# MLP matmuls in four column tiles wherever a stretch of TensorE work also holds values or sums

## The chip, the cores and the metric

The kernel runs on one core of a Trainium2 chip, in one launch. The metric is the device time of an execution in microseconds (us). Engines are named as in the profile: PE is TensorE's matmul, PEld its weight load, ACT is ScalarE, DVE is VectorE, POOL is GpSimd, SP is SyncE.

## The reference

Attention with a few extra "beacon" keys, then an MLP with a gate. There are 8 batches of 8 heads, 576 positions, 16 beacon keys and head size 64; the MLP goes from 512 to 2048 and back to 512 over 4608 tokens. Inputs and the output are float32.

```
scores = q @ concat(beacon_k, k)^T / 8        # causal over k, beacons always seen
a      = exp(scores - max) / (sum + 1e-9)
x      = a @ concat(beacon_v, v)              # per head, then heads side by side: [4608, 512]
h      = x @ w_in
out    = (h * sigmoid(1.702 * h)) @ w_out
```

## The kernel before, in words

All matmul operands are float16. Attention is worked in 16 sets of four heads (`NSET`; a set is half of a batch's heads). The MLP is worked in 10 groups of tokens: two of 256 and eight of 512 (`GROUPS`).

**Three shapes of the array.** TensorE takes a matmul's stationary operand as rows x columns of the array, which the profile prints in front of the moving operand's shape:

- scores (`e_qk`, L434), mode "r": 32 rows by 128 columns. The four heads of a set lie in four groups of 32 partitions, so that four such matmuls fill the array.
- values and sums (`e_av`, L521), mode "c": 128 rows by 32 columns. The four heads write four groups of 32 output partitions of one PSUM tile, so that four such matmuls, a set, fill the array. Sums use a tile of ones as their weights.
- MLP, mode "m": 128 rows by 128 columns. The first layer (`e_m1`, L580) has 512 moving columns in the groups of 512 tokens (256 in the first two groups and where a group crosses the end of the ring buffer `xT`). The second layer is `e_m2` (L625, 512 columns) in the first two groups, and `e_prod` (L694, 256 columns) in the eight others, where it is seven products of quarter matrices that DVE adds up (`e_s`, L645, before; `e_join`, L710, after).

**Order of the work.** Every operation, such as one score visit or one tile of the MLP, is an `Op` of a planner, with its engine, its dependencies and its mode. The order on each engine is written out by hand in the lists `ORDER`; `Plan.run` only merges these lists by start times that it reckons, and hands out the four PSUM tiles `u` as they come free. The function's last loop then emits the operations in that order. There are 55 score visits on TensorE; the scores have a single PSUM tile (`s`), so a visit has to wait until ACT has taken the exponential of the visit before (`e_exp`, L445). Between two visits TensorE works on MLP operations, on values and sums, or on both.

**Around it.** POOL and DVE mask the exponentials (L466, L459), DVE adds parts of the sums up (L484), turns sums into reciprocals (`e_z1`, `e_z2`, L533 to L544) and scales the values into `xT` (`e_norm`, L556). DVE also transposes q and k for the scores (`e_turn`, L405). ACT applies the gate to the first layer (`e_gelu`, L601; in the first two groups tanh on ACT, L594, and DVE, L613). POOL issues the loads, SP the stores.

Of the kernel before, what the change touches and what calls it, by code (L numbers as in the profile page):

```python
# [195 lines left out]
def kernel(  # L196
# [11 lines left out]
    nc = tc.nc  # L208
# [7 lines left out]
    P = 128  # L216
# [8 lines left out]
    NKT = DMODEL // P  # L225
    NNT = DFF // P
# [21 lines left out]
    HM, HN = 256, NNT // 2  # L248
# [71 lines left out]
    for s in range(EARLY, NSET):  # L320
        c = 0
# [14 lines left out]
    def ring_tile(key):  # L336
        if key not in rings:
            i = plan.tiles[key]
            rings[key] = psu.tile([P, 512], F32, tag=f"u{i}", name=f"u{i}")
        return rings[key]  # L340
# [225 lines left out]
        GROUPS.append((t, min(NTOK, t + 512)))  # L566
    NG = len(GROUPS)

    def e_m1(g, n0, n1):
        t0, t1 = GROUPS[g]  # L570
        w = t1 - t0
        if g not in gts:
            gts[g] = gp.tile([P, NNT, 512], F16, tag="g", name="g")
        u = ring_tile(("m1", g, n0))
        for nt in range(n0, n1):
            o = (nt - n0) * w
            cut = max(t0, t1 // XR * XR)
            for a, e in ((t0, cut), (cut, t1)):
                for kp in range(NKT if a < e else 0):
                    nc.tensor.matmul(  # L580
                        u[:, o + a - t0 : o + e - t0],
                        w1t[:, kp, nt * P : (nt + 1) * P],
                        xT[:, kp, a % XR : (e - 1) % XR + 1],
                        start=(kp == 0),
                        stop=(kp == NKT - 1),
                    )

    sigs = {}
# [33 lines left out]
    def e_m2(g, mt, qt):  # L622
        o = ring_tile(("m2", g, mt))
        for nt in range(4 * qt, 4 * qt + 4):
            nc.tensor.matmul(  # L625
                o[:, :],
                gts[g][:, nt, mt * P : (mt + 1) * P],
                w2t[:, nt, :],
                start=(nt == 0),
                stop=(nt == NNT - 1),  # L630
            )

    osbs = {}
# [13 lines left out]
    def tb(i):  # L647
        if i < 3:
            return tB[i][:, :, :]
        return w2t[:, 0:HN, HM:]  # L650
# [14 lines left out]
    def quarter(g, i, j):  # L665
        return gts[g][:, HN * j : HN * (j + 1), HM * i : HM * (i + 1)]
# [13 lines left out]
    def e_prod(g, p, n0, n1):  # L680
        u = ring_tile(("p", g, p))
        w = lambda i, j: w2t[:, HN * i : HN * (i + 1), HM * j : HM * (j + 1)]
        lhs, rhs = {
            1: (quarter(g, 0, 0), w(0, 0)),
            2: (quarter(g, 0, 1), w(1, 0)),
            3: (sA[2], w(1, 1)),
            4: (quarter(g, 1, 1), tb(2)),
            5: (sA[0], tb(0)),
            6: (sA[1], tb(1)),
            7: (quarter(g, 1, 0), tb(3)),  # L690
        }[p]
        for n in range(n0, n1):
            for mt in range(2):
                nc.tensor.matmul(  # L694
                    u[:, HM * mt : HM * (mt + 1)],
                    lhs[:, n, mt * P : (mt + 1) * P],
                    rhs[:, n, :],
                    start=(n == 0 and mt == 0),
                    stop=(n == HN - 1 and mt == 1),
                )  # L700

    def e_half(g, p, dst):
# [236 lines left out]
    def products(g):  # L939
# [17 lines left out]
        def prod(p):  # L957
            prev = []
            for n0 in range(0, HN, SQ):
                deps = list(prev)  # L960
                if lhs[p] is not None:
                    deps.append(sd[(lhs[p], n0)])
                else:
                    deps += [gates[(g, n + (HN if p in (2, 4) else 0))] for n in range(n0, n0 + SQ)]
                if rhs[p] is not None:
                    deps.append(tds[rhs[p]])
                o = op(
                    "PE", 2 * SQ * 109, deps, lambda n0=n0: e_prod(g, p, n0, n0 + SQ), kind="m2", pr=g,
                    ring=("p", g, p), mode="m", name=f"m2.{g}.{p}.{n0}",
                )  # L970
                prev = [o]
            last[p] = prev[0]
            done.setdefault(g, []).append(prev[0])
# [31 lines left out]
    def mlp(g):  # L1005
# [16 lines left out]
        for n0 in firsts:  # L1022
            n1 = n0 + n
            key = ("m1", g, n0)
            pe = op(
                "PE", 4 * n * (w / 2.4 + 2.8), xs + w1_of[n0] + old, lambda n0=n0, n1=n1: e_m1(g, n0, n1),
                kind="m1", pr=g, ring=key, mode="m", name=f"m1.{g}.{n0}",
            )
            m1s.setdefault(g, []).append(pe)
            if g >= GEL:  # L1030
                gates[(g, n0)] = op(
                    "ACT", 480, [pe], lambda n0=n0, n1=n1: e_gelu(g, n0, n1),
                    pr=1, closes=key, name="gelu", table="g",
                )
                continue
            a = op(
                "ACT", 480, [pe] + tanhs[-1:] + gated[-3:-2], lambda n0=n0, n1=n1: e_tanh(g, n0, n1),
                pr=1, name="tanh", table="e",
            )
            tanhs.append(a)  # L1040
            gates[(g, n0)] = op(
                "DVE", 606, [a], lambda n0=n0, n1=n1: e_gate(g, n0, n1), pr=2, closes=key, name="gate"
            )
            gated.append(gates[(g, n0)])
# [3 lines left out]
        for mt in range(w // P):  # L1048
            key = ("m2", g, mt)
            prev = None  # L1050
            for qt in range(4):
                deps = [gates[(g, n0)] for n0 in range(0, NNT if mt else 4 * qt + 4, n)] + [w2_ld[qt], prev]
                prev = op(
                    "PE", 4 * 215.8, deps, lambda g=g, mt=mt, qt=qt: e_m2(g, mt, qt), kind="m2",
                    pr=g, ring=key, mode="m", name=f"m2.{g}.{mt}.{qt}",
                )
                m2s[(g, mt, qt)] = prev
            done.setdefault(g, []).append(prev)
            ev = op("ACT", 480, [prev], lambda g=g, mt=mt: e_evac(g, mt), pr=1, closes=key, name="evac")
            op("SP", 60, [ev], lambda g=g, mt=mt: e_store(g, mt), name="store")  # L1060
# [20 lines left out]
    def also(o, d):  # L1081
        o.deps.append(d)
        o.left += 1
        d.users.append(o)

    for o in done.get(NPL - 1, []) + done.get(NPL - 2, []) if tds else ():
        also(tds[3], o)
    order = plan.run()
    for o in order:
        o.emit()  # L1090

# [28 lines left out]
```

The softmax here doesn't subtract the row's maximum and nothing guards it: scores larger than these inputs give would overflow.

## Time and profile before

| | |
|---|---|
| time, median of 3 runs | 330.57 us (330.24 to 332.09) |
| span of the profiled execution (first to last instruction) | 328.1 us; the profile gives no other time for it |
| TensorE matmuls and weight loads | 4288 each |
| of these: scores, values and sums, MLP | 1376, 1248, 1664 |
| mean granted TensorE clock | 1.000 |
| L580, first layer: busy, count | 130.4 us, 704 |
| ACT's gate L601: busy, count | 70.5 us, 128 |
| ACT's exponential L445: busy, count | 98.9 us, 66 |

The span runs from the first instruction to the last; a run's time is somewhat longer than the span. "Busy" is the union of an engine's instructions. The records of TensorE's matmuls overlap, since one streams in while the last drains and their ends are modelled: a matmul's cost is read from the distance to the next one's start, not from its duration. In the chain of work that ended last, each piece was released by the one before it.

### The profile page before, as it was taken

How to read it: one execution, taken by the hardware profiler on the slowest of the kernel's cores; microseconds unless marked ns; L12 is line 12 of the kernel's file. 1: busy time of each engine (PE TensorE's matmuls, PEld its weight loads, DVE VectorE, ACT ScalarE, POOL GpSimd, SP SyncE). 2: the span in 40 equal slices, each digit the busy share in tenths (PEclk: the TensorE clock that was granted, in tenths of full speed). 3: DMA queues.
4: the chain of work that ended last, by engine and by line, in shares of the span. 5: the costliest groups of instructions: out<-in, count | busy, mean ns of one | idle time of the engine just before them, and what ended most of it. 6: DMA issues, size and time to landing. Idle time of an engine off the chain costs nothing.

```text
span 328.1 us, 9811 instructions
## 1 busy us (share of the span) xinstructions
PE 309.3 (94%) x4288; PEld 210.0 (64%) x4288; DVE 235.9 (72%) x478; ACT 202.0 (62%) x236; POOL 114.0 (35%) x178
## 2 busy tenths in 40 slices
PE   0489999999999999999999999999999999999995
PEld 0367665544775467745878878547764776447884
DVE  3657788777987989977998798958557843006674
ACT  1567597687767686679767686868477212674010
POOL 8765487190319312951078019400042000000000
PEclk9999999999999999999999999999999999999999
DMA  7999999194424921693029809600120012000122
GB/s 126 161 202 209 203 187 181 34 99 103 113 67 72 186 50 34 70 191 57 2 45 177 133 2 122 157 0 2 37 96 2 2 34 78 18 0 2 65 98 97
DMA packets 58219, 28.81 MB, mean 88 GB/s; under 512 B 41280, under 2 KB 53568, under 8 KB 58176
## 3 DMA queue, kind: packets, MB, share of 16 engines
q0 software_dynamic: 47552, 18.49, 47.8%
q1 hardware_dynamic: 10560, 9.69, 9.1%
q8 instruction: 33, 0.54, 0.7%
q14 instruction: 10, 0.08, 0.1%
q10 hardware_dynamic: 64, 0.01, 0.0%
HBM read 37.22 MB, written 9.44 MB: 142 GB/s over the span
## 4 chain that ended last, share of the span: by engine, by line
PE 89%; ACT 4%; DVE 3%; DMA 2%; issue 1%; POOL 0%; DVEq 0%; ACTq 0%; POOLq 0%
PE u L580 36%; PE u L694 30%; PE s L434 9%; PE u L521 9%; PE u L625 4%; ACT E L445 3%; DMA qn<-in_q_dram 2%; DVE qT L405 1%; DVE sA L645 1%; DVE xT L556 1%; DVE rz L544 0%; DVE zt L533 0%; ACT L601 0%; DVE osb L710 0%; DVE rc L540 0%
## 5 line engine op out<-in xcount | busy, mean ns | idle before, releaser
L580 PE MATMUL u<-xT,w 128*128 128x512 f16 (+1 forms) x704 | 130.4, 340 | 0.5 <-ACT g L601 0.5
L445 ACT ACTIVATE E<-s 128x2048 f16<-128x2048 f32 (+5 forms) x66 | 98.9, 1515 | 46.0 <-PE s L434 45.6
L601 ACT ACTIVATE g<-u 128x512 f16<-128x512 f32 x128 | 70.5, 598 | 53.8 <-PE u L580 53.4
L580 PEld LDWEIGHTS <-w 128*128 128x128 f16 x704 | 67.8, 98 | 53.9 <-issue 1.5
L466 POOL TENSOR_SCALAR_AFFINE_SELECT E<-E 128x512 f16<-128x512 f16 (+3 forms) x78 | 49.3, 663 | 113.4 <-ACT E L445 81.6
L710 DVE SCALAR_TENSOR_TENSOR osb<-u,osb 128x512 f32<-128x512 f32 x56 | 37.2, 682 | 24.7 <-PE u L694 22.4
L694 PEld LDWEIGHTS <-g 128*128 128x128 f16 x512 | 48.4, 98 | 9.3 <-issue 0.2
L694 PE MATMUL u<-w,g 128*128 128x256 f16 x384 | 50.6, 273 | 0.0
L434 PE MATMUL s<-qT,kT 32*128 32x32 f16 (+20 forms) x1376 | 35.4, 232 | 14.4 <-DVE qT L405 8.4
L434 PEld LDWEIGHTS <-kT 32*128 32x128 f16 x1376 | 25.8, 94 | 30.6 <-issue 15.0
L694 PEld LDWEIGHTS <-sA 128*128 128x128 f16 x384 | 36.3, 98 | 5.3 <-issue 0.3
L694 PE MATMUL u<-tB,sA 128*128 128x256 f16 x256 | 35.0, 273 | 0.1
L645 DVE TENSOR_TENSOR sA<-g 128x512 f16<-128x512 f16 x32 | 12.9, 415 | 26.2 <-ACT g L601 26.2
L556 DVE TENSOR_TENSOR xT<-u,rz 128x352 f16<-128x352 f32 (+2 forms) x52 | 25.6, 517 | 6.9 <-PE u L521 6.7
L365 POOL DMA_DIRECT2D vb<-in_v_dram x32 | 27.4, 874 | 2.3 <-DMA kn<-in_k_dram 1.5
L521 PE MATMUL u<-E,vb 128*32 128x352 f16 (+8 forms) x928 | 28.0, 267 | 0.0
L484 DVE TENSOR_TENSOR zs<-zs,E 128x1344 f16<-128x1344 f16 (+2 forms) x36 | 22.7, 633 | 5.3 <-POOL E L466 4.4
L521 PEld LDWEIGHTS <-vb 128*32 128x32 f16 (+1 forms) x928 | 20.2, 99 | 5.9 <-issue 1.7
L405 DVE STREAM_TRANSPOSE kT<-kn 128x576 f32<-128x576 f32 x16 | 20.1, 1258 | 2.4 <-DMA kn<-in_k_dram 1.6
L405 DVE STREAM_TRANSPOSE qT<-qn 128x576 f32<-128x576 f32 x16 | 19.8, 1239 | 0.1
L533 DVE STREAM_TRANSPOSE zt<-u 128x224 f32<-128x224 f32 (+2 forms) x32 | 14.9, 471 | 6.6 <-PE u L521 6.5
L484 DVE TENSOR_TENSOR zs<-E 128x1856 f16<-128x1856 f16 x12 | 15.8, 1319 | 3.3 <-POOL E L466 3.3
(44 smaller groups left out, 237.7 us busy)
## 6 DMA issues: line engine op xcount, KB each, us to landing
out_dram<-osb SPq DMA_DIRECT2D x36, 256.0 KB, 2.5
kn<-in_k_dram POOLq DMA_DIRECT2D x16, 288.0 KB, 6.7
qn<-in_q_dram POOLq DMA_DIRECT2D x16, 288.0 KB, 6.6
vb<-in_v_dram POOLq DMA_DIRECT2D x24, 128.0 KB, 6.6
w<-in_moe_w_in_dram POOLq DMA_DIRECT2D x8, 256.0 KB, 9.9
w<-in_moe_w_out_dram POOLq DMA_DIRECT2D x4, 512.0 KB, 14.2
vb<-in_v_dram POOLq DMA_DIRECT2D x8, 112.0 KB, 5.0
vb<-in_v_dram POOLq DMA_DIRECT2D x8, 80.0 KB, 7.9
```

What stands on the lines that cost most here:

```text
L365: nc.gpsimd.dma_start(out=t[0 : hi - lo, j, h0:h1, :], in_=v[b, h0:h1, lo:hi, :].rearrange("h n d -> n h d"),)
L405: nc.vector.transpose(out=f32(dst.rearrange("p n e -> p (n e)")).rearrange("p (r t) -> p t r", t=TR), in_=f32(src[:, :]).rearrange("p (t c ...
L434: nc.tensor.matmul(sc[:, h, o : o + w], kT[s % NB2][r : r + 32, j * P : (j + 1) * P, d], qT[s % NB2][r : r + 32, a : a + w, d], start=(d = ...
L445: nc.scalar.activation(out=Es[s][:, :, c0:c1], in_=ss[i][:, :, o : o + c1 - c0], func=AFT.Exp, scale=0.125,)
L466: nc.gpsimd.affine_select(out=blk, in_=blk, compare_op=ALU.is_ge, fill=0.0, base=off + (Nb if j == 0 else 0), pattern=[[0, Q], [1, w]], ch ...
L484: nc.vector.tensor_tensor(out=t, in0=E[:, :, Z0:S] if i == 1 else t, in1=E[:, :, wcol[i] : wcol[i] + S - a], op=ALU.add,)
L521: nc.tensor.matmul(u[32 * h : 32 * h + 32, a:e], lhs, src[0:kw, h, col : col + e - a], start=first, stop=last,)
L556: nc.vector.tensor_tensor(out=xT[:, 2 * hs + x : 2 * hs + x + n, t0 : t0 + w], in0=rings[("av", s, x, half)][:, 0 : n * w].rearrange("p (n ...
L580: nc.tensor.matmul(u[:, o + a - t0 : o + e - t0], w1t[:, kp, nt * P : (nt + 1) * P], xT[:, kp, a % XR : (e - 1) % XR + 1], start=(kp == 0) ...
L601: nc.scalar.activation(out=gts[g][:, n0:n1, 0:w], in_=rings[("m1", g, n0)][:, 0 : n * w].rearrange("p (n w) -> p n w", n=n), func=AFT.Gelu ...
L694: nc.tensor.matmul(u[:, HM * mt : HM * (mt + 1)], lhs[:, n, mt * P : (mt + 1) * P], rhs[:, n, :], start=(n == 0 and mt == 0), stop=(n == H ...
L710: nc.vector.scalar_tensor_tensor(out=osbs[(g, dst)][:, :], in0=rings[("p", g, p)][:, :], scalar=scale_of(g), in1=osbs[(g, src)][:, :], op0 ...
```

## The change

MLP matmuls go through a new helper `mm`. With its flag set, it issues one matmul as four, one for each group of 32 output partitions: the weights' columns are cut into four, and each part meets the same moving operand. The flag is set for an MLP operation if the stretch of TensorE's order between two score visits in which it stands holds values or sums too (mode "c"). The work behind the last score visit counts as one such stretch. All else is emitted as before, in the same order.

```diff
+    tiled = [False]
+
+    def mm(o, lhs, rhs, start, stop):
+        if not tiled[0]:
+            nc.tensor.matmul(o, lhs, rhs, start=start, stop=stop)
+            return
+        for r in range(0, P, 32):
+            nc.tensor.matmul(o[r : r + 32], lhs[:, r : r + 32], rhs, start=start, stop=stop)
+
...
-                    nc.tensor.matmul(
+                    mm(
                         u[:, o + a - t0 : o + e - t0],
                         w1t[:, kp, nt * P : (nt + 1) * P],
                         xT[:, kp, a % XR : (e - 1) % XR + 1],
-                        start=(kp == 0),
-                        stop=(kp == NKT - 1),
+                        kp == 0,
+                        kp == NKT - 1,
                     )
...
     order = plan.run()
+    split, visit = set(), []
+    for o in [o for o in order if o.eng == "PE"] + [None]:
+        if o is None or o.mode == "r":
+            if any(x.mode == "c" for x in visit):
+                split.update(x.seq for x in visit if x.mode == "m")
+            visit = []
+        else:
+            visit.append(o)
     for o in order:
+        tiled[0] = o.seq in split
         o.emit()
```

The matmul calls in `e_m2` (L625) and `e_prod` (L694) are put through `mm` in the same way.

More of the change, by code (lines that the diff above doesn't have):

```diff
@@ L624, in e_m2 @@
         for nt in range(4 * qt, 4 * qt + 4):
-            nc.tensor.matmul(
+            mm(
                 o[:, :],
@@ L628, in e_m2 @@
                 w2t[:, nt, :],
-                start=(nt == 0),
-                stop=(nt == NNT - 1),
+                nt == 0,
+                nt == NNT - 1,
             )
@@ L693, in e_prod @@
             for mt in range(2):
-                nc.tensor.matmul(
+                mm(
                     u[:, HM * mt : HM * (mt + 1)],
@@ L697, in e_prod @@
                     rhs[:, n, :],
-                    start=(n == 0 and mt == 0),
-                    stop=(n == HN - 1 and mt == 1),
+                    n == 0 and mt == 0,
+                    n == HN - 1 and mt == 1,
                 )
```

## The prediction

> **What bounds the kernel now.** I read the page's busy rows and slices first, then its chain of work that ended last, then the timeline of TensorE alone, then the waits that TensorE ends.
>
> ```profile
> span 328.1 us, 9811 instructions
> ...
> PE 309.3 (94%) x4288; PEld 210.0 (64%) x4288; DVE 235.9 (72%) x478; ACT 202.0 (62%) x236; POOL 114.0 (35%) x178
> ...
> PE   0489999999999999999999999999999999999995
> ...
> PEclk9999999999999999999999999999999999999999
> ...
> PE 89%; ACT 4%; DVE 3%; DMA 2%; issue 1%; POOL 0%; DVEq 0%; ACTq 0%; POOLq 0%
> ```
>
> TensorE is busy in every slice after the first two, at the full granted clock, and 89% of the chain is TensorE work. A change in TensorE's time therefore reaches the end nearly one for one, except where another engine already holds TensorE up. The timeline of TensorE shows what the change touches:
>
> ```profile
> 130.87 0.60 PE L694 MATMUL u<-tB,sA 128*128 128x256 f16 x4
> 131.40 0.64 PE L434 MATMUL s<-qT,kT 32*128 32x384 f16 x24
> 131.97 1.61 PE L521 MATMUL u<-E,vb 128*32 128x224 f16 x56
> 133.51 1.05 PE L694 MATMUL u<-tB,sA 128*128 128x256 f16 x8
> 134.49 0.65 PE L434 MATMUL s<-qT,kT 32*128 32x320 f16 x24
> ...
> 150.19 4.49 PE L580 MATMUL u<-xT,w 128*128 128x512 f16 x20
> 154.52 1.04 PE L694 MATMUL u<-w,g 128*128 128x256 f16 x8
> 155.49 0.38 PE L521 MATMUL u<-zs,ones 128*32 128x352 f16 x8
> 155.69 0.23 PE L521 MATMUL u<-E,ones 128*32 128x80 f16 x8
> 155.85 0.61 PE L694 MATMUL u<-tB,g 128*128 128x256 f16 x4
> ```
>
> The first column is the start; the second column's end includes a modelled pipeline tail, so I use differences of starts. Three shapes of the array take turns: scores (L434, 32*128), values and sums (L521, 128*32) and MLP (L580, L625, L694, 128*128). Record by record, successive MLP matmuls of one run start 109 ns apart at 256 columns and 216 ns at 512: columns / 2.4 plus 2.5 ns.
>
> **What a change of shape costs.** From 154.52, eight MLP matmuls last 8 x 109 = 874 ns, but L521 starts after 970: 96 ns for the change. Over the whole trace the 15 changes from MLP to values cost 93 to 94 ns each, and the first set behind one runs 10 ns over its usual pitch: 104. From values to MLP (26 changes) it is 94 to 98 ns behind the fourth matmul of the last set (one is 106), and the first MLP matmul's pitch is 10 ns long as well: 107. Check on the 56 at 131.97: 14 sets of four with 3,328 columns are 1,387 ns at 2.4 columns per ns, some 44 for 14 pitches and 10 for the first; L694 starts after 1,540, so 99 are left, plus the 10.
>
> **Part 1, changes removed.** Following TensorE's timeline from end to end, there are 52 stretches between score visits with other work; 28 hold both MLP and values or sums, and inside these are the 41 changes above. They all go: 15 x 104 + 26 x 107 = 4.3 us. The changes at the two ends of a stretch stay (85 to 97 ns in every combination). In 20 of the 28 the last work is MLP; its fourth column tile now starts 10 ns behind its first, as L521's does: +0.2 us. Gross: **4.1 us**.
>
> **Part 2, matmuls added.** The 28 stretches hold 1,188 of the 1,664 MLP matmuls (404 of 512 columns, 784 of 256), among them all 408 behind the last values, where no change of shape is left to save. Each becomes four of 32 output rows: 3,564 matmuls and as many weight loads more. The nearest row is L521, which already runs this shape. Its four matmuls of a set start within 10 ns, and the next set starts columns / 2.4 plus 2 to 3 ns later: 149 to 150 ns at 352, 89 at 208, 49 at 112. The MLP pitch is columns / 2.4 plus 2.5. I take **0** per matmul. Not shown by any row: 512 columns in this shape, four tiles that read the same moving rows, and hundreds of sets in a row. The bound below is 0.5 ns less (0.6 us in all), the lower end of L521's 2 to 3 ns; above, the sets that follow an 80-column one (5 to 7 ns over, so +5 each, 5.9 us), and the supply of instructions, priced below as a rival. I take 0 because the sets of 208 to 352 columns are the nearest in width.
>
> Weights: four loads per set instead of one. In the 112-column sets four loads hide inside 49 ns, so they hide inside 109. If that cover failed, the 60 ns of room in a 256-column set would be the first to go.
>
> A rule against this change: the Trainium skill, "TensorEngine Tiling (Array Packing)", section Instruction Overhead, gives each matmul some 60 cycles of overhead and advises tiling for small dimensions only, which the MLP has not. Summed over four at 2.4 GHz that is an estimated 100 ns per set; were it added to the stream rather than hidden, 75 ns more for each of 1,188 matmuls, 89 us. The 49 ns sets of four say that it isn't added.
>
> Semaphores: in L521's sets only the fourth matmul carries the update; I expect the same, at no cost. The order of all engines is fixed by the ORDER lists and the planner's inputs are untouched, so no DMA, queue or buffer moves. The score operations, ACT, DVE and POOL instructions are the same.
>
> **Part 3, savings that another wait takes.** A score visit has one PSUM tile, so it cannot start before the last exponential ended. Where it did wait, it starts 51 or 52 ns after that end; where it starts later than that, the difference is slack.
>
> ```profile
> 83.01 0.55 DVE rz L544
> ...
> 86.69 0.44 DVE xT L556
> 87.14 0.04 issue
> 87.18 1.03 PE u L694 x8
> ...
> 91.75 1.89 ACT E L445
> 93.63 0.04 issue
> 93.67 0.65 PE s L434 x21
> ```
>
> In these pieces of the chain, ACT sets the start at 93.67: both changes saved in the stretch before it (0.21 us) only lengthen that wait. Scores at 49.59, 99.35, 102.11 and 195.73 start 111, 117, 195 and 84 ns after their exponential, 60, 65, 145 and 33 of slack against savings of 105, 105, 210 and 105: 0.22 us lost. Elsewhere behind mixed stretches the slack covers the saving. The DVE chain up to 87.18 starts from values at 80.9, so the two changes between are lost too (0.21). At 37.24 the scores wait for DVE's transposition of q; the change of shape behind the last values before it is lost, and DVE's idle 0.17 us ahead of that chain caps two more: together 0.2. Sum: **0.85 us** taken back, 3.3 left. At the end, six changes sit in the last stretch, from 241 on, where no other engine holds TensorE for more than 0.1 us; the last DVE join and the store follow as before.
>
> **Sum.** 328.1 - 3.3 = 324.8 us of span. The profile gives that execution no other time than its span; the median of the runs is 330.57, 2.5 more, for what lies around it. 324.8 + 2.5 = **327.3 us**, 1.0% faster.
>
> **Rivals.**
> *Waits take it back.* DVE is busy 36.5 of 40 us from 100 to 140, and the median slack ahead of a score visit is about 250 ns. If tighter waits on DVE and ACT absorb everything before 241, six changes remain: 0.6 us, 330.0. For it: the five clipped visits. Against: TensorE's own waits sum to under 2 us after 20.
>
> *Slower: the supply of instructions.* A 256-column set now takes 8 instructions in 109 ns, 13.6 ns each, through stretches as long as 11 us. The densest 256 instructions on record took 4.27 us from 56.5, 16.7 ns each. If that were the ceiling, a set would take 133 ns: 24.4 x 784 = 19 us more, less 3.3: 346. The 512-column sets (27 ns each) stay clear. It decides the sign from 13.6 + 3300 / 784 / 8 = 14.2 ns per instruction. Against it: TensorE's closing drain was reached with 33 instructions still to start, so some 33 are queued ahead; 192 instructions in 2.14 us from 229.3 then needed (192 - 33) per 2.14 us, 13.5 ns, and 128 in 1.05 us from 164.3 needed 11.1, and no set was late. Fetching shows here:
>
> ```profile
> q8 instruction: 33, 0.54, 0.7%
> ```
>
> 33 packets of 16 KB, 256 instructions each, took 0.9 to 1.8 us apiece; in the new stretches one is due every 3.5 us. During the fetch at 53.3, 77 instructions started in its 0.98 us.
>
> *Slower by a little: each set costs more,* for one of the reasons that no row shows, at the upper bound of 5 ns: 5.9 - 3.3 = +2.6, 333.2. Break-even is 3.3 us / 1,188 = 2.8 ns.
>
> *It doesn't do what it says:* the split MLP still drains against L521 because something other than the shape sets the drain. L521's 80-row sets behind 128-row ones show none (+2 ns). It would give 330.57 + 0.2: 330.8.
>
> **Chances.** Forecast 0.58; absorbed 0.14 (within 0.5%); instruction supply 0.15 (slower); a few ns per set 0.10, half of it within 0.5%, half slower; no effect 0.03 (within). So faster by over 0.5% 0.58, within 0.5% 0.22, slower 0.20; 0.5% is about what a measurement of this kernel tells from no change. The range goes from 326.4, the whole gross of 4.1 us (the 0.6 us of the lower bound beyond it I hold unlikely), to 333, which leaves out the supply rival and the far tails, some 0.19.
>
> **What would show it.** TensorE 7,852 matmuls and as many loads; MLP groups of shape 128*32; starts of L694 sets 109 to 110 ns apart; 41 gaps of some 95 ns gone; waits for ACT before scores at 49.6, 93.7, 99.4, 102.1 and 195.7 longer by up to 0.2 us. Wrong if the L694 sets stand 113 ns or more apart, with idle time put down to issue (supply) or evenly spread (cost per set), or if the gaps between L694 and L521 stay.

## The result and the profile after

The changed kernel takes **340.82 us** (median of 6 runs, 339.75 to 342.37) against 330.74 (329.77 to 332.10): a ratio of **1.0306**, 95% interval 1.0278 to 1.0334. It is slower by 10.1 us; the forecast was 3.3 us faster, and the time lies beyond the range.

The page of the changed kernel, the lines that answer to those shown of before:

```profile
span 339.1 us, 16939 instructions
...
PE 308.1 (91%) x7852; PEld 228.6 (67%) x7852; DVE 236.1 (70%) x478; ACT 202.5 (60%) x236; POOL 114.1 (34%) x178
...
PE   0486889999999999998997699999999999999995
...
PEclk9999999999999999999999999999999999999999
...
q8 instruction: 61, 1.00, 1.2%
...
PE 81%; DVE 7%; ACT 5%; issue 4%; DMA 2%; POOL 1%; SPq 1%; DVEq 0%; ACTq 0%
```

TensorE has the 7,852 matmuls expected and is busy for 1.2 us *less* than before, in a span that is 11 us longer. Slices 4 to 6, 19, 22 and 23 of its row (8.48 us each) have 6, 7 or 8 where before had 9, and "issue" has grown from 1% to 4% of the chain. The clock is the same.

First what was forecast and came. TensorE's timeline of the changed kernel, the stretch that was shown at 131.97 of before:

```profile
137.05 1.61 PE L521 MATMUL u<-E,vb 128*32 128x224 f16 x56
138.49 1.05 PE L576 MATMUL u<-tB,sA 128*32 128x256 f16 x32
139.47 0.65 PE L434 MATMUL s<-qT,kT 32*128 32x320 f16 x24
```

From the 56 matmuls of values to the MLP it is now 1.44 us instead of 1.54: the change of shape is gone. The eight MLP matmuls, now 32, take 0.98 us up to the scores, as before. Record by record, a set of four starts columns / 2.4 plus 2 to 3 ns before the next, in the median of all set pitches at 256 and at 512 columns; between MLP and values, either way round, nothing is left of the 95 ns but for one wait (for DVE, at 143.67).

Then what came beside it. Lines of the same timeline, from four places, show how TensorE stops in the middle of a run:

```profile
25.83 0.39 PE L573 MATMUL u<-xT,w 128*128 128x256 f16 x2
27.75 1.69 PE L573 MATMUL u<-xT,w 128*128 128x256 f16 x14 [1.53 <-issue]
...
46.09 0.19 PE L434 MATMUL s<-qT,kT 32*128 32x32 f16 x2 [1.24 <-issue]
...
180.35 1.58 PE L521 MATMUL u<-E,vb 128*32 128x352 f16 x52
183.70 0.22 PE L521 MATMUL u<-E,vb 80*32 80x80 f16 x4 [1.77 <-issue]
...
190.18 1.06 PE L576 MATMUL u<-xT,w 128*32 128x256 f16 x32 [2.87 <-issue]
```

The bracket is idle time and what ended it; "issue" means that no semaphore did. The stops strike split MLP (190.18), values (183.70), scores (46.09) and an MLP run that wasn't split at all (27.75, still 128*128). There are ten of them. I counted TensorE's records up to each (weight loads, matmuls and the few drain and semaphore records, four by the first stop and eleven by the last), and set beside it the packet of the instruction queue (q8) that came last:

| last start to next start (us) | records before it | q8 packet (us) | restart after the packet's end |
|---|---|---|---|
| 25.95 to 27.75 | 705 | 25.49 to 26.45 | 1.30 |
| 32.00 to 33.68 | 961 | 31.41 to 32.31 | 1.38 |
| 38.07 to 39.61 | 1217 | 37.20 to 38.09 | 1.52 |
| 44.68 to 46.09 | 1473 | 43.68 to 44.74 | 1.35 |
| 154.42 to 155.57 | 6593 | 153.33 to 154.31 | 1.26 |
| 178.00 to 178.45 | 7873 | 175.81 to 176.94 | 1.51 |
| 181.68 to 183.70 | 8129 | 181.07 to 182.14 | 1.55 |
| 187.03 to 190.17 | 8385 | 187.94 to 188.90 | 1.27 |
| 193.59 to 193.91 | 8641 | 191.65 to 192.63 | 1.28 |
| 332.23 to 332.78 | 15553 | 330.56 to 331.43 | 1.35 |

Every count is 193 more than a multiple of 256, and 256 instructions are one packet of 16 KB. TensorE stands where a block of its instructions ends, until 1.3 to 1.6 us after the next block's packet has ended. In the kernel before, it enters no block sooner than 1.9 us after that block's packet, and no border has a stop. From last start to next start the ten add up to 14.1 us, **13.4 us** beyond the usual pitch (the expectations below say 13.6). The sum, from the records of TensorE's starts in both profiles (after minus before; a gap goes from the first start of a run's last set to the next run's first start): gaps from values to MLP -2.24, from MLP to values -1.40, at the ends of stretches +1.16; starts within runs of MLP +8.68, of values +3.18, within score visits +1.58; together 11.0, as much as TensorE's last start came later. The three terms within runs make 13.4, as much as the stops.

When is a block asked for? Where TensorE has just starved, the moment it enters a block is known to the ns, and so is the start of the next packet. With the DMA engines all but idle in between, it started 1.18 us (entered at 155.57), 1.19 (193.91) and 1.09 (332.78) later; with the loads running (a busy share of 1.2 to 2.2; packets under way side by side add up to more than 1), 3.66 (27.75), 3.52 (33.68), 4.07 (39.61), 2.62 (178.45) and 4.24 (183.70); twice, with loads for part of the time, it was 1.48 and 2.23. It fits that a block is asked for on entering the block before it and that its packet queues behind loads. From entering one block to the next being usable, that makes an estimated 1.1 + 1.0 + 1.4 = 3.5 us when it is quiet; under load it was 5.2 to 6.5, from one restart to the next (27.75, 33.68, 39.61 and 46.09; 178.45, 183.70 and 190.17). A block of 256-column sets lasts 32 x 109 ns = 3.5 us; before, a block of such matmuls lasted four times as long.

### The profile page after: what moved, and what is told of

Read it like the earlier page. It is cut to its first block, busy times and chain, and to the rows that moved or that the text cites. A ratio compares the mean times of both kernels' runs of the same rounds, so it can differ in the third digit from the quotient of the medians.

```text
span 339.1 us, 16939 instructions
## 1 busy us (share of the span) xinstructions
PE 308.1 (91%) x7852; PEld 228.6 (67%) x7852; DVE 236.1 (70%) x478; ACT 202.5 (60%) x236; POOL 114.1 (34%) x178
## 4 chain that ended last, share of the span: by engine, by line
PE 81%; DVE 7%; ACT 5%; issue 4%; DMA 2%; POOL 1%; SPq 1%; DVEq 0%; ACTq 0%
PE u L576 48%; PE u L573 17%; PE u L521 8%; PE s L434 8%; ACT E L445 3%; DMA bkf<-in_beacon_k_dram 2%; DVE sA L654 1%; DVE zs L484 1%; DVE osb L719 1%; ACT g L610 1%; POOL E L466 1%; DVE rz L544 1%; DVE g L654 1%; SPq L384 1%; DVE xT L556 1%
## 5 line engine op out<-in xcount | busy, mean ns | idle before, releaser
L576 PE MATMUL u<-xT,w 128*32 128x512 f16 (+1 forms) x2208 | 105.2, 344 | 5.0 <-issue 4.3
L576 PEld LDWEIGHTS <-w 128*32 128x32 f16 x2208 | 62.7, 97 | 39.3 <-issue 6.4
L576 PE MATMUL u<-w,g 128*32 128x256 f16 (+1 forms) x1296 | 47.2, 284 | 1.2 <-issue 1.2
L576 PEld LDWEIGHTS <-g 128*32 128x32 f16 x1616 | 43.8, 97 | 6.0 <-issue 1.6
L573 PE MATMUL u<-xT,w 128*128 128x512 f16 (+1 forms) x152 | 26.8, 329 | 1.5 <-issue 1.5
L521 PEld LDWEIGHTS <-vb 128*32 128x32 f16 (+1 forms) x928 | 21.4, 99 | 7.2 <-issue 3.1
L576 PEld LDWEIGHTS <-sA 128*32 128x32 f16 x928 | 25.0, 97 | 1.3 <-issue 0.9
L573 PEld LDWEIGHTS <-w 128*128 128x128 f16 x152 | 14.6, 98 | 12.2 <-issue 2.0
L576 PE MATMUL u<-tB,sA 128*32 128x256 f16 x576 | 20.4, 273 | 0.3 <-issue 0.3
L573 PE MATMUL u<-w,g 128*128 128x256 f16 (+1 forms) x124 | 20.4, 297 | 0.0
```

The lines of the kernel that those rows point to most:

```text
L521: nc.tensor.matmul(u[32 * h : 32 * h + 32, a:e], lhs, src[0:kw, h, col : col + e - a], start=first, stop=last,)
L573: nc.tensor.matmul(o, lhs, rhs, start=start, stop=stop)
L576: nc.tensor.matmul(o[r : r + 32], lhs[:, r : r + 32], rhs, start=start, stop=stop)
```

## The experiments

Theory **S** (supply) is that paragraph. Its rival **R** is that the tiles themselves cost time in long runs. All ratios are to the kernel before; unless said otherwise the edit is to the changed kernel.

**Where the DMA engines are quiet, and where they are filled on purpose.**

```diff
 e1_tail_only
-            if any(x.mode == "c" for x in visit):
-                split.update(x.seq for x in visit if x.mode == "m")
+            if o is None:
+                last = max(n for n, x in enumerate(visit) if x.mode == "c")
+                split.update(x.seq for x in visit[last:] if x.mode == "m")
 e2_tail_and_loads (this added to e1), e3_loads_only (this added to the kernel before)
+    last_c = [o for o in order if o.mode == "c"][-1]
     for o in order:
         ...
         o.emit()
+        if o is last_c:
+            for n in range(72):
+                e_load_qk(n % 6, n // 6 % 2)
```

> Only the 408 MLP matmuls behind the last values are issued as four column tiles, nothing else; one change of shape (0.1 us) goes. Theory S (supply): TensorE's instructions come in blocks of 256, the next block is asked for when the stream enters the one before, and TensorE stands still where it runs through a block sooner than the next arrives, which is so where DMA engines are busy with loads; here they are nearly quiet, so one stall of about 0.5 us and 330 to 331.5 us, no different from before. Theory R (the shape): the tiles themselves cost time in long runs, wherever they are; 408 of 1188 matmuls then bring a third of the 13.6 us of unexplained standing time, about 4.7 us, and the time is about 335.

> As the run with the tail alone split, and 72 loads of q and k (288 KB each) that nobody reads are issued by POOL once it is done with its own work, to fill the DMA engines from about 240 us on. S: blocks of 256-column sets take 3.5 us and fetches under load 4.6 to 6.7, so several stalls of 1 to 3 us, all at block borders: 4 to 16 us over the same loads without the split. R: the same difference to its partner as the tail alone has to before.

> The kernel before with the same 72 loads that nobody reads, no matmul split: the control for the run before it. S and R: within 1 us of before, unless the loads themselves delay the stores at the end; in S no stall at block borders, since a block lasts 14 us or more there.

Measured: e1 331.59 us, 1.0044 (1.0010 to 1.0078); e2 391.33, 1.1844 (1.1796 to 1.1893); e3 390.75, 1.1826 (1.1777 to 1.1876). The loads outlast all else in e2 and e3, which I had not seen coming, so their times don't answer; TensorE's last start does: 324.54 in e1, **339.13** in e2, **324.67** in e3, 323.96 in before. The busy shares of two windows within the split end, of e1 and then of e2 (engines' busy time and count, clock, DMA share, GB/s):

```profile
300.00:323.00 23.00, 23.00 (x804) 21.84 (x800) 14.61 (x33) 3.41 (x6) 0.00 (x0) 1.00 0.19 62
```

```profile
300.00:337.00 37.00, 26.50 (x871) 23.31 (x867) 18.11 (x41) 4.18 (x7) 10.13 (x21) 1.00 1.05 193
```

With a DMA share of 0.19, 408 split matmuls run without a stop, even the one of about 0.5 us that S expected; with 1.05, TensorE is busy for 26.5 of 37 us. From e2's timeline:

```profile
308.40 0.61 PE L576 MATMUL u<-w,g 128*32 128x256 f16 x13 [1.32 <-issue]
314.60 0.61 PE L576 MATMUL u<-tB,g 128*32 128x256 f16 x13 [2.52 <-issue]
325.07 0.61 PE L576 MATMUL u<-w,g 128*32 128x256 f16 x13 [2.10 <-issue]
330.71 1.92 PE L576 MATMUL u<-w,g 128*32 128x256 f16 x61 [1.97 <-issue]
336.91 2.64 PE L576 MATMUL u<-w,sA 128*32 128x256 f16 x45 [2.52 <-issue]
```

Seven stops in all, 13.6 us from last start to next start (as in all sums of stops below), all at records 193 beyond a multiple of 256. In e3, the same loads and no split, there is none. R expected e2 to differ from e3 by what e1 differs from before; it falls. e1's own 0.4% is a little more than I expected: in its profile TensorE ends 0.6 us later, and 0.4 of that is there by the end of the opening, which the edit does not touch.

**The late loads left out.**

```diff
 e5_split_no_late_loads; the same two edits to the kernel before are e6_no_late_loads
-        ... lambda: e_load_qk(s, which), due=due, ...
+        ... lambda: e_load_qk(s, which) if s < 2 * HS else None, due=due, ...
-            ... lambda: e_load_v(b, j, 0, H),
+            ... lambda: e_load_v(b, j, 0, H) if b < 2 else None,
```

> The changed kernel without the loads of q, k and v for batches 2 to 7 (their sets compute on what the first two batches left), so that the DMA engines are quiet from some 30 us on but for the weights and stores. S: the standing time at block borders after 60 us (7.1 us in the changed kernel) falls below 1 us and some of the 6.1 us before 60 us goes too; the gaps saved stay saved, so it is 0 to 4 us over its partner without the split instead of 10. R: still about 10 us over its partner.

> The kernel before without the same loads: the partner. S and R: within 1.5 us of before, as TensorE seldom waits for a load there.

Measured: e5 335.26 us, 1.0135 (1.0103 to 1.0168); e6 330.69, 1.0003 (0.9982 to 1.0024). The split costs 4.6 us instead of 10.1; S had said 0 to 4. The DMA slices of e5's page, 8.3 us each, show the first six still full, and then no more than stores:

```profile
DMA  7999970000301101110012001200111011100222
```

The four stops before 60 us are there as in the changed kernel (6.4 us), which S had not expected; those after it have shrunk from 7.6 to 1.0 us, two stops of 0.39 and 0.60 at 180 and 184. So a block of dense work only just lasts in quiet times, and the loads make the rest. That the stops before 60 us did not shrink fits their DMA slices, which are full in both.

**The early stretches alone.**

```diff
 e10_early_only (n_visit counts the stretches; the 16th starts at 66 us)
-            if any(x.mode == "c" for x in visit):
+            if n_visit < 16 and any(x.mode == "c" for x in visit):
```

> All MLP matmuls of mixed stretches before 66 us are split, none later. S: the four stalls of 1.4 to 1.8 us at block borders between 25 and 47 us, under the first loads, come back, 6.1 us, less about 1 us for the changes of shape: 335 to 336. R: 108 of 1188 matmuls are a tenth of 13.6 us, less 1: no slower than before.

Measured: 335.42 us, 1.0140 (1.0094 to 1.0186), the number that S expected. Three of the four stops are there, at records 961, 1217 and 1473, 4.5 us, for which R has no place. But the agreement is in part luck. In its profile TensorE's last start comes 5.6 us later than before: 4.5 from the stops, 0.9 saved at changes of shape, and 2.0 by 25 us that no stop made. Most of these 2.0 are in 16 unsplit matmuls, in this run and then in the changed kernel:

```profile
21.50 3.11 PE L573 MATMUL u<-xT,w 128*128 128x256 f16 x16
```

```profile
20.69 1.92 PE L573 MATMUL u<-xT,w 128*128 128x256 f16 x16
```

Up to 23.8 us they start 213 ns apart, not 109, at half the usual rate. The first entry of the granted clock in this trace stands at 24.0 us (17.7 in before, 18.0 in the changed kernel, 19.0 in e1, 19.3 in e8), which fits a clock not yet at full; but the views print 1.00 there, so the cause stays open. Late as it was, TensorE came to record 705 at 28.3, 1.6 us after its packet, and did not stop there.

**More instructions without column tiles.**

```diff
 e11_pieces_and_loads (from e2)
-        for r in range(0, P, 32):
-            nc.tensor.matmul(o[r : r + 32], lhs[:, r : r + 32], rhs, start=start, stop=stop)
+        w = rhs.shape[-1] // 4
+        for c in range(0, 4 * w, w):
+            nc.tensor.matmul(o[:, c : c + w], lhs, rhs[:, c : c + w], start=start and c == 0, stop=stop and c == 3 * w)
```

> The 408 matmuls at the end are cut in four along the moving columns instead, with the full array and the same weights loaded four times, so that the number of instructions grows without column tiles; the 72 loads that nobody reads run beside them. S: TensorE stands at block borders, until 1.2 to 1.6 us after the fetch ended, as with column tiles; by as much, 14 us, if a set still lasts 109 ns, by less if four full weight loads make it longer. R: no standing time at block borders.

Measured once: 395.36 us, again ended by the loads; TensorE's last start is at 338.79. From its timeline, in the shape that before had all along:

```profile
315.36 0.55 PE L577 MATMUL u<-tB,g 128*128 128x64 f16 x13 [2.56 <-issue]
326.11 0.55 PE L577 MATMUL u<-w,g 128*128 128x64 f16 x13 [2.25 <-issue]
337.40 1.63 PE L577 MATMUL u<-w,sA 128*128 128x64 f16 x45 [3.65 <-issue]
```

Six stops, 11.5 us, again at 193 beyond a multiple of 256. The number of instructions does it, not the column tiles: R is refuted.

**Two tiles instead of four.**

```diff
 e8_two_tiles
-        for r in range(0, P, 32):
-            nc.tensor.matmul(o[r : r + 32], lhs[:, r : r + 32], rhs, start=start, stop=stop)
+        for r in range(0, P, 64):
+            nc.tensor.matmul(o[r : r + 64], lhs[:, r : r + 64], rhs, start=start, stop=stop)
```

> The same MLP matmuls as two column tiles of 64 output rows instead of four of 32. If only the values' own shape spares the change, all 41 gaps of some 95 ns stay, with half the added instructions: S then gives a few stalls under load and 331 to 334. If any column tiling spares it, 4 us go and few stalls come: 327.5 to 329.5. R: half of 13.6 us, less the saving or not.

Measured: 331.71 us, 1.0022 (0.9997 to 1.0047). From its timeline:

```profile
133.20 1.61 PE L521 MATMUL u<-E,vb 128*32 128x224 f16 x56
134.74 1.06 PE L576 MATMUL u<-tB,sA 128*64 128x256 f16 x16
```

1.54 us again from the values to the MLP, and all 41 gaps stay, at 94 to 106 ns: column tiles of 64 save nothing beside column tiles of 32. The Trainium skill, "TensorEngine Tiling (Array Packing)", section Key Properties, says that a change of tiling mode, not of tile, drains TensorE; this row agrees, with some 108 ns. There is one stop at a block border, 0.38 us, under the early loads; another 0.7 us of its profile's 1.6 lies between the scores of the opening.

**Fewer splits.** The changes of shape are saved by run: a run of MLP work between values and scores saves one whatever its length, so short runs save as much for fewer instructions.

```diff
 e4_short_runs, e7_where_quiet, e9_chosen: runs of one mode within a stretch, then
+                if run[0].mode == "m" and "c" in beside and sum(x.dur for x in run) <= LIMIT:
+                    split.update(x.seq for x in run)
 e4: LIMIT = 2200
 e7: LIMIT = 20000 if n_visit >= 46 else 1000
 e9: LIMIT = 20000 if n_visit >= 46 else 2200 if n_visit in (22, 26, 27, 32, 35, 44) else 0 if n_visit in (17, 20) else 1000
```

> Split only runs of MLP work of at most 2.2 us (by the planner's durations) that touch values or sums: most of the changes of shape go, with some 300 instead of 1188 matmuls split. S: the saving of about 2.4 us shows in the gaps; a stall or two under the early loads takes part of it back: 328.5 to 330.5. R: 300 / 1188 of 13.6 us is 3.4 us, less 2.4: about 331.5.

> Split only runs of up to 1 us that touch values or sums, and from the stretch at 222.8 us on also longer ones, without the 408 matmuls at the end: where blocks last longest or the DMA engines are quiet. S: some 15 changes of shape go and hardly a stall comes: 1.0 to 1.6 us faster, 329 to 329.6. R: 200 split matmuls cost 2.3 us and save 1.5: 331.3.

> The split where it was quiet, plus six more runs of up to 2.2 us (in the stretches at 97, 123, 126, 149, 165 and 205 us) and without those at 82 and 92 us, whose saving another wait takes. S: six more changes of shape go, 0.6 us more than the 1.0 us of the run before, if no block border falls badly: 328.7 to 329.3. R: 60 more split matmuls cost what they save: 329.5.

Measured: e4 331.55 us, 1.0024 (1.0001 to 1.0047); e7 **329.54**, 0.9969 (0.9946 to 0.9991); e9 **329.27**, 0.9965 (0.9936 to 0.9995). e4 splits 244 matmuls (5,020 in all, less 4,288, by three) and has three stops at block borders, 2.4 us, two of them before 61 us under the early loads; that is more than I allowed for, and beyond its 328.5 to 330.5. R's 331.5 was met, though by stops at block borders and not by the tiles. e7 splits 188 and e9 268, with no stop at all, and both are faster than before by about 1 us, so faster than both kernels of this study. e9's six further changes of shape were to give another 0.6; its time lies within 0.3 of e7's and inside its interval, and tells nothing between S and R; e7 lies 1.8 below R's number. In its profile the gaps between MLP and values are 1.7 us smaller than before in sum, e7's 1.3, so part of what it saved was met by other waits, as in part 3 of the prediction.

## Why the prediction was wrong, point by point

- **What bounds the kernel: right.** The loss is all TensorE's, and the other engines' busy times hardly moved (DVE 235.9 to 236.1, ACT 202.0 to 202.5).
- **Part 1, changes removed: right, at nearly its size.** The gaps between MLP and values fell by 3.6 us, and by 4.0 when the 0.35 us that one wait for DVE put into them (at 143.67) is taken out; 4.1 was the forecast with the first pitches.
- **Part 2, the matmuls: right** in all that was called unshown. 512 columns, four tiles on the same moving rows and long runs have the same pitch, and loads of weights hide. "A few ns per set" was wrong as a rival.
- **Part 2, the supply of instructions taken at 0: this is the step that failed.** It was priced as a rival at 0.15, with 19 us, by a rate per instruction; it came, with 13.4 us, by another law, a time per block. I had shown that 128 and 192 instructions were supplied at 11 to 13.5 ns each. But those lie in blocks that had arrived over 4 us earlier, and say nothing of how long the next takes. And I held the packet's 0.9 to 1.8 us against the 3.5 us of a block, without the 1.1 us that pass before a packet starts in quiet times, the 2.6 to 4.2 under load and the 1.3 to 1.6 behind it. With them the sum reads 3.5 against 3.5 in the quiet, which is no cover, and 5.2 to 6.5 against 3.5 under load, a stop of up to 3 us at a border. Nor are the 33 instructions queued ahead a fixed number: the changed kernel reached its closing drain with 46 still to start. The fetches under load were in the trace of before; I read how long they took and not how late they came.
- **Part 3, savings that other waits take: right in kind.** The gaps at the ends of stretches, most of them ahead of scores, grew by 1.2 us in sum, and the wait for DVE took 0.35 (0.85 forecast).
- **The sum** with the missing term: 327.3 + 13.4 = 340.7, measured 340.8. That it closes so well is in part luck: in the profiled pair the gaps gave 0.8 us less than forecast (3.6 - 1.2 against 3.3), but that pair's spans lie 11.0 us apart and the medians only 10.1. The 2.5 us "around" the span are not all around it: a run of 340.84 us has a span of 339.1, so 1.7 are, and the profiled execution of before was faster than the median.
- **The range** left out the rival that happened, and its chance was too low. The rule that was weighed, 60 cycles added to each matmul, was rightly put aside: four column tiles have the pitch of one whole matmul. (The page's advice on small dimensions stands in its section When to Use Tiling, not in the one named.)

The Trainium skill has the fetch: "Runtime: NRT & Kernel Launch", section Instruction fetch mechanics, says that instructions come in blocks of 16 KB, 256 of them, by the engine's own DMA queue while the block before is run, and calls the cost of a border mostly hidden. The packets agree with the block; the ten stops do not agree with "hidden" once a block lasts under some 3.5 us, or 5.2 to 6.5 under load.

## What to carry to other kernels

Before cutting TensorE's work into more and smaller instructions, work out how long 256 of them last, and compare it with the time from entering one block to having the next: here some 3.5 us with quiet DMA engines, 5.2 to 6.5 with loads running. A change of array shape cost 95 ns and some 10 more, whatever the number of matmuls that it takes to avoid it, so spend instructions only on the short runs and outside the loads. An average rate over a window shorter than a block proves nothing about fetching.

## What the runs showed of the hardware beyond that

- A stop at a block border strikes whatever stands there: at 27.75 an MLP run in the old shape stood 1.5 us for instructions that split work ahead of it (64 matmuls from 23.0 on) had used up.
- The loads delay instruction packets by waiting time, not by transfer time: nine of the ten packets in the table took 0.88 to 1.07 us, one 1.13, while the wait for their start went from 1.1 to 4.2.
- Loads that nobody waits for can so cost time: in e3 the 72 loads moved TensorE's last start by 0.7 us against before, in e2, with four times the instructions, by 14.6 against e1.
